# State products in 64x64 tiles from lasting token-major K buffers, with a new order of work

## The chip, the cores and the metric

One core of a Trainium2 chip runs the program. The metric is the device time of one execution in microseconds. Times are medians of repeated runs; the profile is one further execution.

## The reference

A complex gated recurrence over 768 tokens, for 4 batches and 8 heads of 48 features, feeds a gated feed-forward block that mixes tokens with a 768x768 matrix:

```python
def _attn_ref(q, k, v, a_re, a_im):            # each (4, 8, 768, 48)
    B, H, S, D = q.shape
    mag = np.sqrt(a_re * a_re + a_im * a_im)
    scale = np.minimum(mag, 0.999) / (mag + 1e-06)
    a_re_n, a_im_n = (a_re * scale, a_im * scale)
    for t in range(S):                         # S_re, S_im: (B, H, D, D), start at zero
        ar, ai = (a_re_n[:, :, t, :, None], a_im_n[:, :, t, :, None])
        new_re = ar * S_re - ai * S_im
        new_im = ar * S_im + ai * S_re
        kv = np.einsum('bhd,bhe->bhde', k[:, :, t], v[:, :, t])
        S_re, S_im = (new_re + kv, new_im)
        y[:, :, t] = np.einsum('bhd,bhde->bhe', q[:, :, t], S_re)
    return y

def _moe_ref(x, w_in, g_ln, w_sg, b_sg, w_out):   # x (4, 768, 384)
    h = gelu_tanh(x @ w_in)                       # w_in (384, 1024)
    u, v = (h[..., :512], h[..., 512:])
    v_n = (v - mean(v)) / np.sqrt(var(v) + 1e-06) * g_ln
    v_s = np.einsum('ts,bsd->btd', w_sg, v_n) + b_sg[None, :, None]   # w_sg (768, 768)
    return x + (u * v_s) @ w_out                  # w_out (512, 384)
```

## The kernel before

**The recurrence in chunks.** Each batch is cut into six chunks of 128 tokens, counted g = 0 to 23 over the four batches. The gates become logarithms and angles that are summed over time; then k and q are scaled and rotated with the sums, so that within a chunk the recurrence is a masked product of k and q, and across chunks a state of 96x48 numbers for each head (cosine and sine half of 48 features). Chunks are prepared in units of one or two: units 0 to 3 are batch 0, units 4 to 12 are the three units of each of the batches 1 to 3.

**The chains.** Each piece of work is a Python generator that issues one step of instructions at every `yield`. Of a unit n: `l`, `m` (loads of the gates; of k and q), `g` (`logs`), `e` (`scale`), `t` (`arctan`), `p` (`turns`), `s` (`sincos`). Of a chunk g: `v` (load of V into `vbuf[g % 2]`), `r` (`rotate`, line 557), `z` (`heads`, line 582), `c` (`tokens`, line 608), `d` (`states`, line 623), `a` (`attend`, line 653). Of the feed-forward block, for a batch b and a group of token chunks from c0: `nb_c0` (`normal`: x times the second half of `w_in` into `pv`, gelu, normalization), `xb_c0` (`expand`: the first half into `pu`, gelu), `yb_c0` (`spatial`: `w_sg` into `pvs`, gating, `w_out` into `po`, output). `w` prepares weights, `h` and `k` read gates and weights once more for a range check, `f` issues warming products into a tile that nobody reads (line 225), `o0`, `o1` and `ok` are constants, vectors and the end of the check.

**The order.** `ORDER` (line 32) is a table of tokens. `g2:3` calls the chain g2 three times; an apostrophe or two behind a token sets `alt`, which chooses the engine where a step has a choice: an elementwise step runs on GpSimd with one apostrophe and else on VectorE (`ew`, line 203); a copy out of PSUM on ScalarE without, on VectorE with one or two (`evac`, line 207); a rounding on ScalarE, GpSimd or VectorE (`high`, line 213); warming products are 0, 1 or 3. Every engine executes its instructions in the order of this table, and SyncE issues the DMAs in that order, each when what it needs is there. Nearly all DMAs are on SyncE's queue.

**From rotation to state, batches 1 to 3.** Data are feature-major. `rotate` makes two products for k and two for q (cosine and sine, lines 573 to 580) and writes each to DRAM (`rk`, `rq`). `heads` reads them back head by head into tiles `K` and `Q` of 96 rows, in four DMAs for a unit: K and Q of heads 0 to 3, K and Q of heads 4 to 7. `tokens` transposes K to token-major, four heads at a time into the PSUM tile `pk` (line 618), and copies it into a pool tile `kt` (line 620), of which there are two. In batch 0 data are token-major from the start: `rotate` writes `k0` into the same pool, and `heads` transposes.

**`states`** multiplies, for each head and each half of 64 tokens, K (64x96, stationary) by V (64x48) into `ps`; the two halves go to two PSUM tiles, and the last chunk of a batch needs the first half only (line 630). VectorE adds the older state (`Sm`, `S`), and `ew` scales the result (line 649). **`attend`** makes K times Q in tiles of 96x64 into `pa` (line 665), masks it to `am`, multiplies V by it in 64x64 tiles into two tiles `py` (line 680; row half, then column half, in turn), adds the states' part (line 689), copies `py` to `yp` (line 692) and writes it to DRAM. PSUM tiles `ps`, `pk`, `pa` and `py` share one pool of four banks (`pst`); the feed-forward block has three banks (`psm`).

Products of fp32 data show as two records on TensorE, those of rounded fp32 (fp32r) data as one; a transpose shows as one.

Of the kernel before, what the change touches and what calls it, by code (L numbers as in the profile page):

```python
# [37 lines left out]
w4 l4 g3 r2' g3:2 w5 a1:2 a0 r2'' w5:2 a1' a1 r3' m3 a1'' w12 w4 e3 g4 w4' w5 m3 w12 e3:2 e3' e3 z3 z3' z2 g4 z3 z2 z3
e3'' e3 z2:2 l6 a1 w12 p3 z2:4 v3 g4' p3' w12 g4 e3' e3 p3 d2:2 a2 d2 g4 a2 a2'' e3' t4 z3 z3'' z3 g4 p3:2 a2 p3:2
n0_0 v4 w12' a2 z3 l5 a3 n0_0' a3 a2 d2' p4:3 a2 d3 a2' a2 d3:2 n0_0' s3 a3' s3:2 w8 r5'' a3 r4 r4' a3 a3' a3 g4:2 g5  # L40
z5:2 z4 z4' z4 a3 z4:3 v5 r5' g4 d3' z4 z4'' e3 p4 z5:3 z5' p4 z5 a3 w3'' g5 o0 w11 e4 m4 z5' a5 a4' p4 l5 w8:2' a4 m4
n0_2 w12'' a4 d4' a5 d4 e4'' e4 a4 w3' s4:3 r6 e3 g5' g5 d4 n0_0 t5 e4' d4' w6 e4 r6 r6'' r6 a4 a4'' a4 d5 a4' a5''
# [20 lines left out]
d15 a15 d14' g11 v17 d15:2 g11:2 a15:4 z16:2 g11 z16:2 m10 g10 e10 y1_0 y1_3'' y1_3 c16 y1_3 c17 g11 c17' c17 c16''
c17' y1_3 a15 c16 c16' m10 x1_0 y1_3 e10'' y1_3 p10 y1_3 p10 y1_3 p10 y1_3 e10 y1_3 a16:3 d16 a16 d15 d16 n2_0 d16
s10:3 e9 a17 a16 a16' a17 e9'' a17'' a16 y1_0 d16' d17'' t11 d17'' r18'' a16 p11 a16 n2_0 r18 v18 a17:2 a17'' r18''
a17:3 h0 e10' p11 r18 n2_0' e10 r18'' r18 h0 r18' r18 p11 g11 y1_0 y1_0'' p11 y1_0' y1_0:2 g11 n2_3 h16 y1_0 z18 y1_0
# [968 lines left out]
```

## Time and profile before

| | us |
|---|---|
| runs of the kernel | 529.76, 521.91, 519.26; median 521.91 |
| profiled execution, its own time | 517.86 |
| its span, first to last instruction | 516.1 |
| TensorE busy | 459.8 |
| VectorE busy | 386.3 |
| ScalarE busy | 289.5 |
| GpSimd busy | 223.4 |

The span lies inside the execution's own time. Busy times are sums over the span, and a busy TensorE isn't TensorE at its peak, since its products are pipelined. In the rows, PE is TensorE, DVE VectorE, ACT ScalarE, POOL GpSimd and SP SyncE; L635 is line 635 of the kernel; `a<-b,c` names what is written and read.

### The profile page before, as it was taken

How to read it: one execution, taken by the hardware profiler on the slowest of the kernel's cores; microseconds unless marked ns; L12 is line 12 of the kernel's file. 1: busy time of each engine (PE TensorE's matmuls, PEld its weight loads, DVE VectorE, ACT ScalarE, POOL GpSimd, SP SyncE). 2: the span in 40 equal slices, each digit the busy share in tenths (PEclk: the TensorE clock that was granted, in tenths of full speed). 3: DMA queues.
4: the chain of work that ended last, by engine and by line, in shares of the span. 5: the costliest groups of instructions: out<-in, count | busy, mean ns of one | idle time of the engine just before them, and what ended most of it. 6: DMA issues, size and time to landing. Idle time of an engine off the chain costs nothing. (4 is left out here: it accounts for less than half of the span.)

```text
span 516.1 us, 11823 instructions
## 1 busy us (share of the span) xinstructions
PE 459.8 (89%) x4824; PEld 410.2 (79%) x4824; DVE 386.3 (75%) x607; ACT 289.5 (56%) x388; POOL 223.4 (43%) x250
## 2 busy tenths in 40 slices
PE   7799789879796989979898989999999969999995
PEld 4456677669695978868788989788999959889995
DVE  4999999996992966848878958889786823656644
ACT  7897779576975764395467463567755310253000
POOL 6447697667526025545616004547441312332102
PEclk9999789879896995989879999997999976999999
DMA  6885546891275784581671875977745793554232
GB/s 192 236 254 141 161 126 185 242 261 64 77 228 141 232 209 157 167 265 53 210 215 43 256 220 142 296 224 234 225 154 158 232 227 105 155 185 151 70 103 80
DMA packets 64148, 91.30 MB, mean 177 GB/s; under 512 B 9940, under 2 KB 49110, under 8 KB 64088
## 3 DMA queue, kind: packets, MB, share of 16 engines
q1 hardware_dynamic: 63944, 90.29, 59.2%
q8 instruction: 39, 0.64, 0.5%
q14 instruction: 21, 0.17, 0.1%
q10 hardware_dynamic: 144, 0.20, 0.1%
HBM read 66.87 MB, written 23.60 MB: 175 GB/s over the span
## 5 line engine op out<-in xcount | busy, mean ns | idle before, releaser
L197 ACT ACT_TABLE_LOAD x65 | 83.4, 1283 | 2.0 <-PEq L1020 0.9
L234 PE MATMUL pvs<-wsgh,vh 128*128 128x384 f32 x192 | 67.6, 352 | 2.8 <-DVE vh L220 2.8
L234 PE MATMUL pvs<-wsgh,vl 128*128 128x384 f32 x192 | 66.5, 346 | 0.2
L234 PE MATMUL pvs<-wsgl,vh 128*128 128x384 f32 x192 | 66.3, 345 | 0.0
L234 PEld LDWEIGHTS pvs<-wsgh,vh 128*128 128x128 f32 x192 | 37.4, 195 | 3.5 <-DVE vh L220 3.0
L618 PE MATMUL pk<-ident,K 96*128 96x96 f32 x144 | 20.0, 284 | 22.3 <-DMA K<-rk 22.3
L665 PE MATMUL pa<-Q,K 96*64 96x64 f32 x768 | 34.5, 251 | 5.4 <-DMA Q<-rq 4.7
L665 PEld LDWEIGHTS pa<-Q,K 96*64 96x64 f32 x768 | 30.4, 163 | 10.2 <-issue 4.2
L234 PEld LDWEIGHTS pvs<-wsgh,vl 128*128 128x128 f32 x192 | 37.4, 195 | 0.9 <-DVE vl L223 0.8
L234 PEld LDWEIGHTS pvs<-wsgl,vh 128*128 128x128 f32 x192 | 37.4, 195 | 0.0
L618 PEld LDWEIGHTS pk<-ident,K 96*128 96x128 f32 x144 | 16.2, 163 | 26.1 <-issue 15.1
L635 PE MATMUL ps<-vbuf,kt 64*96 64x48 f32 x528 | 34.3, 274 | 1.8 <-DVE kt L209 1.6
L635 PEld LDWEIGHTS ps<-vbuf,kt 64*96 64x96 f32 x528 | 31.9, 189 | 4.4 <-DVE kt L209 2.2
L234 PE MATMUL pu<-xh,winh 128*128 128x384 f32 x96 | 34.0, 354 | 0.6 <-DVE tg L818 0.6
L234 PE MATMUL pv<-winh,xh 128*128 128x512 f32 x72 | 31.9, 442 | 2.4 <-DVE tg L818 1.3
L805 PE MATMUL po<-gh,wouth 128*128 128x384 f32 x96 | 33.8, 352 | 0.0
L805 PE MATMUL po<-gl,wouth 128*128 128x384 f32 x96 | 33.2, 345 | 0.0
L805 PE MATMUL po<-gh,woutl 128*128 128x384 f32 x96 | 33.1, 345 | 0.0
L234 PE MATMUL pu<-xl,winh 128*128 128x384 f32 x96 | 33.1, 345 | 0.0
L234 PE MATMUL pu<-xh,winl 128*128 128x384 f32 x96 | 33.1, 345 | 0.0
L198 ACT ACTIVATE vr<-pv 128x512 f32<-128x512 f32 x24 | 14.4, 599 | 32.3 <-PE pv L234 25.8
L218 POOL TENSOR_SCALAR gh<-tg 128x384 fp32r<-128x384 f32 x14 | 8.2, 584 | 52.6 <-DVE tg L821 47.6
(290 smaller groups left out, 1262.0 us busy)
## 6 DMA issues: line engine op xcount, KB each, us to landing
K<-rk SPq DMA_DIRECT2D x18, 384.0 KB, 6.3
Q<-rq SPq DMA_DIRECT2D x18, 384.0 KB, 7.5
x<-xd SPq DMA_DIRECT2D x9, 576.0 KB, 5.6
vbuf<-in_v_dram SPq DMA_DIRECT2D x24, 192.0 KB, 2.6
xd<-yp SPq DMA_DIRECT2D x48, 96.0 KB, 2.6
gr<-in_f_re_dram SPq DMA_DIRECT2D x12, 384.0 KB, 3.3
gr<-in_f_im_dram SPq DMA_DIRECT2D x12, 384.0 KB, 4.7
out_dram<-x SPq DMA_DIRECT2D x23, 192.0 KB, 2.6
```

Of the source, the lines that this page charges most:

```text
L197: nc.scalar.preload_act_table_set(SETS[t])
L198: nc.scalar.activation(out, in_, func, scale=scale, **kw)
L218: nc.gpsimd.tensor_scalar(out=h, in0=src, scalar1=1.0, scalar2=1.0, op0=ALU.mult, op1=ALU.mult)
L234: nc.tensor.matmul(o, w(i), x(i), start=(i == 0 and j == 0), stop=(i == n - 1 and j == 2))
L618: nc.tensor.transpose(pk[:, hh, :], U[n]["K", i, g2][:, hh, :], ident[0:2 * D, 0:2 * D])
L635: nc.tensor.matmul(ps[:, h, :], kh(h)[r], V[r, h * D:(h + 1) * D], start=True, stop=True)
L665: nc.tensor.matmul(pa[r, h, :], K(h)[:, r], Q(h)[:, r], start=True, stop=True)
L805: nc.tensor.matmul(po[d], w[:, f, ds], g[:, f, :], start=f == 0 and j == 0, stop=f == NF - 1 and j == 2)
```

## The change

Token-major K gets two lasting buffers `kbuf`, 800 columns wide: 8 heads of 96 columns and 32 columns of zeros, filled once on GpSimd. `rotate` (batch 0) and `tokens` (other batches) write K of chunk g into `kbuf[g % 2]`. In `states` each product becomes two: the stationary operand is 64 tokens by 64 columns, first columns 0 to 63 of the head, then columns 64 to 127, of which the last 32 belong to the next head (or are the zeros). They go to rows 0 to 63 and 64 to 127 of `ps`, which has 128 rows; the adds read the first 96. `ORDER` is a new table over the same chains, with other apostrophes. Of the table, the diff shows the first lines and those around the unit 12 (chunks 22 and 23).

```diff
--- before.py
+++ after.py
@@ -30,57 +30,56 @@
 ORDER = """
-l0 g0 l0 g0 g0'' f'' w13 o0:2 g0 w0 g0 g0' t0 p0 g0:2 l2 w0:2 w13 w0 p0' p0 w13 s0 w13 e0 p0 l1 g1 l1 g1 g1'' w2:2
...
-a20 s12 a21 y2_3:7 d21 a21:2 d21 a21:3 y2_0 k3 y2_3:2 r22'' r22 a21 e12:2 x2_0 d21 r22:2 r22' r22 y2_0 r22' x2_0 r22
-v23 y2_0'' y2_0 y2_0'' n3_0 y2_0:2 d21 y2_0'' y2_0:2 z22 h22 f h14 f:5 h14 f y2_0:2 y2_0:2' y2_0:2 z22:2 h23:2 c22:2
-x2_0 z22 c22:2 c23 h21 c23'' c23:2 a22:3 d22 d23' d22:2 e12 h21 a22 k5 h11 h4 k5 e12' a23 x2_0 a23 a22 n3_0 a23 a22:4
...
+l0 g0 l0 w13 f' g0 g0'' g0:2 t0 o0:2 w13:2 f' w13 f g0' f'' w13'' f w0:4 w0:2'' g0:2 f' l1:2 p0:2 e0 w13'' p0:2 g1:2
...
+y2_3 v23 y2_3:7 r22' y2_3 e12' x2_0:6 e12 h21 y2_0 n3_0 h21 r22 r22'' r22 r22'' r22 r22'' r22 z22:4 y2_0 y2_0' y2_0''
+y2_0' y2_0 x2_0 h6 y2_0 y2_0'' y2_0 y2_0'' y2_0:2 h5 y2_0:2 y2_0'' x2_0 y2_0:2 a21:2 c22 c22'' c23 c22 c22'' c23:3 h5
+a22:2 e12 d22 a22'' a22:2 e12' y2_0 d22 a23 n3_0' d22 n3_0' a22' a23 a22 d22 d23' h13 a23'' a23:2 a22:2 h15 y2_0 d23'
...
 """

@@ -171,6 +170,11 @@
     for i in range(2):
         vbuf.append(cst([P, DM + 64 - D], F32, f"vbuf{i}"))
         nc.gpsimd.memset(vbuf[i][:, DM:], 0.0)
+    kbuf = []
+    for i in range(2):
+        kbuf.append(cst([P, 2 * DM + P - 2 * D], F32, f"kbuf{i}"))
+        nc.gpsimd.memset(kbuf[i][:, 2 * DM:], 0.0)
+    by_token = lambda g: kbuf[g % 2][:, 0:2 * DM].rearrange("p (h d) -> p h d", d=2 * D)
 
     cuts = SIZES0 + [[UC] * NU] * (B - 1)
     units = [(b, sum(z[:i]), z[i]) for b, z in enumerate(cuts) for i in range(len(z))]
@@ -561,9 +565,9 @@
         if not fea(n):
             by_heads = lambda t: t[:, i].rearrange("p (h d) -> p h d", d=D)
             for nm in "kq":
-                X = (ap_ if nm == "k" else mp).tile([P, H, 2, D], F32, tag={"k": "kt", "q": "x"}[nm], name=nm + "0", bufs=2)
+                X = by_token(g) if nm == "k" else mp.tile([P, H, 2 * D], F32, tag="x", name="q0", bufs=2)
                 u[nm + "0", i] = X
-                ew().tensor_mul(X, by_heads(u[nm]).unsqueeze(2).broadcast_to([P, H, 2, D]),
+                ew().tensor_mul(X.rearrange("p h (a d) -> p h a d", d=D), by_heads(u[nm]).unsqueeze(2).broadcast_to([P, H, 2, D]),
                                 u["csn"][:, :, i].rearrange("p a (h d) -> p h a d", d=D))
                 yield
             return
@@ -589,7 +593,7 @@
                     pk = pst.tile([2 * D, 4, P], F32, tag="t", name="pk")
                     stoke(pk[:, 0:2].rearrange("p a b -> p (a b)"))
                     for hh in range(4):
-                        nc.tensor.transpose(pk[:, hh, :], U[n][nm + "0", i][:, 4 * g2 + hh].rearrange("p a d -> p (a d)"), ident)
+                        nc.tensor.transpose(pk[:, hh, :], U[n][nm + "0", i][:, 4 * g2 + hh], ident)
                     yield
                     evac(X[:, 4 * g2:4 * g2 + 4, :], pk)
                     U[n][nm.upper(), i, g2] = X[:, 4 * g2:4 * g2 + 4, :]
@@ -610,8 +614,7 @@
         n, i = at_chunk[g]
         if not fea(n):
             return
-        kt_ = ap_.tile([P, H, 2 * D], F32, tag="kt", name="kt", bufs=2)
-        run["kt", g] = lambda h: kt_[:, h]
+        kt_ = by_token(g)
         for g2 in range(2):
             pk = pst.tile([P, 4, 2 * D], F32, tag="t", name="pk")
             for hh in range(4):
@@ -626,14 +629,17 @@
         c = g % NCH
         last = c == NCH - 1
         V = vbuf[g % 2]
-        kh = run["kt", g] if fea(n) else lambda h: U[n]["k0", i][:, h].rearrange("p a d -> p (a d)")
-        pss = [pst.tile([2 * D, H, D], F32, tag="t", name="ps") for _ in HALVES[:1 if last else 2]]
+        kb = kbuf[g % 2]
+        pss = [pst.tile([P, H, D], F32, tag="t", name="ps") for _ in HALVES[:1 if last else 2]]
         if g < EARLY:
             stoke(pss[0][:, 0:5].rearrange("p a b -> p (a b)"))
         for h in range(H):
             for ps, r in zip(pss, HALVES):
-                nc.tensor.matmul(ps[:, h, :], kh(h)[r], V[r, h * D:(h + 1) * D], start=True, stop=True)
-        yield
+                for w in HALVES:
+                    nc.tensor.matmul(ps[w, h, :], kb[r, h * 2 * D + w.start:h * 2 * D + w.stop], V[r, h * D:(h + 1) * D],
+                                     start=True, stop=True)
+        yield
+        pss = [ps[0:2 * D] for ps in pss]
         Sm = run["Sm", g] = ap_.tile([2 * D, H, D], F32, tag="Sm", name="Sm", bufs=1)
         if c == 0:
             evac(Sm, pss[0])
```

## Rows read from the trace of the kernel before

**Rows 1.** The page: busy time of each engine (us, share of the span, instructions), and the granted TensorE clock in 40 equal slices, in tenths; then span and mean granted clock of the core.

```profile
PE 459.8 (89%) x4824; PEld 410.2 (79%) x4824; DVE 386.3 (75%) x607; ACT 289.5 (56%) x388; POOL 223.4 (43%) x250
PEclk9999789879896995989879999997999976999999
core 0: 516.1 us, clock 0.912
```

**Rows 2.** A stretch of 40 us: its length, busy time (and instructions) of each engine, the granted clock, the DMA share and GB/s.

```profile
40.00:80.00 40.00, 33.42 (x458) 26.20 (x458) 37.61 (x46) 29.75 (x46) 31.12 (x27) 0.87 0.53 152
```

**Rows 3.** Waits, longest first in total: engine and line, what it waited for, us in total, times, longest; and the chain of work that ended last, by line, as shares of the span.

```profile
PE pk L618 <- DMA K<-rk: 22.3, 10, 3.8
PE pk L592 <- DVE yp L209: 4.2, 1, 4.2
by line: PE pvs L234 4.9%; DMA gr<-in_f_re_dram 3.6%; DMA K<-rk 3.2%; PE pu L234 3.2%; PE po L805 3.1%; PE pv L234 2.8%; PE ps L635 1.9%; issue 1.8%; DMA rq<-q 1.7%; PE pa L665 1.5%; DMA x<-xd 1.0%; POOL q L577 0.8%; PE py L689 0.8%; PE pk 
```

**Rows 4.** TensorE's timeline in one attention stage at full clock: start us, us, engine, line, operation, out<-in, shape, number of records.

```profile
308.27 1.15 PE L665 MATMUL pa<-Q,K 96*64 96x64 f32 x32
309.35 1.56 PE L635 MATMUL ps<-vbuf,kt 64*96 64x48 f32 x32
310.84 0.69 PE L680 MATMUL py<-am,vbuf 64*64 64x64 f32 x32
311.47 0.38 PE L493 MATMUL pd<-cols__3420,of_place 128*32 128x16 f32 x18
311.77 0.69 PE L665 MATMUL pa<-Q,K 96*64 96x64 f32 x16
313.75 1.55 PE L635 MATMUL ps<-vbuf,kt 64*96 64x48 f32 x16
315.23 0.69 PE L680 MATMUL py<-am,vbuf 64*64 64x64 f32 x32
```

**Rows 5.** Groups of instructions of TensorE by line and form: the products of `states` of batches 1 to 3 and of batch 0 (number of records | busy us, mean ns | idle before).

```profile
L635 PE MATMUL ps<-vbuf,kt 64*96 64x48 f32 x528 | 34.3, 274 | 1.8 <-DVE kt L209 1.6
L635 PE MATMUL ps<-vbuf,k 64*96 64x48 f32 x176 | 10.4, 253 | 0.9 <-DVE S L646 0.4 <-DVE k L566 0.3
```

**Rows 6.** TensorE's timeline: seven of the ten token transposes that waited for K, with the idle time before them in brackets (units 5, 5, 6, 7, 8, 12, 12).

```profile
157.30 0.55 PE L618 MATMUL pk<-ident,K 96*128 96x96 f32 x4 [1.75 <-DMA K<-rk]
160.79 0.90 PE L618 MATMUL pk<-ident,K 96*128 96x96 f32 x4 [2.95 <-DMA K<-rk]
194.81 1.51 PE L618 MATMUL pk<-ident,K 96*128 96x96 f32 x8 [3.79 <-DMA K<-rk]
228.67 0.90 PE L618 MATMUL pk<-ident,K 96*128 96x96 f32 x4 [3.72 <-DMA K<-rk]
259.08 0.88 PE L618 MATMUL pk<-ident,K 96*128 96x96 f32 x4 [1.70 <-DMA K<-rk]
417.23 0.52 PE L618 MATMUL pk<-ident,K 96*128 96x96 f32 x4 [2.13 <-DMA K<-rk]
422.21 2.15 PE L618 MATMUL pk<-ident,K 96*128 96x96 f32 x12 [2.49 <-DMA K<-rk]
```

**Rows 7.** The chain of work that ended last, in order of time (start us, us, what): four runs of dense products, with their number.

```profile
452.18 6.53 PE pv L234 x27
458.71 6.34 PE pu L234 x36
465.05 3.24 PE pvs L234 x18
486.54 6.33 PE po L805 x36
```

**Rows 8.** Four stretches after waits for K (columns as in rows 2).

```profile
160.00:170.00 10.00, 9.21 (x156) 8.66 (x158) 2.79 (x5) 6.68 (x8) 2.79 (x2) 0.52 0.35 103
194.00:208.00 14.00, 13.19 (x121) 12.75 (x122) 8.92 (x10) 6.45 (x8) 8.30 (x4) 0.53 0.50 167
228.00:235.00 7.00, 6.33 (x50) 5.82 (x50) 2.05 (x3) 4.12 (x6) 2.49 (x7) 0.54 0.69 229
256.00:265.00 9.00, 7.04 (x39) 6.83 (x38) 6.36 (x11) 3.26 (x6) 3.83 (x9) 0.50 0.72 224
```

**Rows 9.** Operations that the change moves or adds to: the copies of `yp` on VectorE and ScalarE and the fills of `vbuf` (ns min/median/max), the scaling of S on GpSimd (busy us, mean ns), and the first warming products (six records, three products).

```profile
L209 DVE COPY yp<-py x30: 392/412/429, 39.9 to 440.3; 128x256 f32<-128x256 f32 x30
L211 ACT COPY yp<-py x18: 351/372/377, 41.6 to 440.3; 128x256 f32<-128x256 f32 x18
L649 POOL TENSOR_TENSOR S<-S,dec 96x384 f32<-96x384 f32 x12 | 12.6, 1047 | 31.9 <-DVE dec L209 28.5 <-DVE S L646 1.9 <-PE pu L234 1.4
L173 POOL MEMSET vbuf<- x2: 114/114/114, 3.3 to 3.3; 128x16 f32 x2
2.82 2.93 PE L229 MATMUL warm<-u_turn,mask 128*128 128x256 f32 x6 [0.25 <-DVE cols L169]
```

**Rows 10.** DMA issues by line: KB each, median us to landing; the read back of K and the write of its second half.

```profile
K<-rk SPq DMA_DIRECT2D x18, 384.0 KB, 6.3
rk<-k SPq DMA_DIRECT2D x9, 384.0 KB, 2.8
```

More of the change, by code (lines that the diff above doesn't have):

```diff
@@ L38 @@
[L38 to L42, printed above, removed]
@@ L63 @@
[L63 to L66, printed above, removed]
-y1_0' y1_0:2 y1_0'' y1_0:2' y1_0:2 y1_0'' z18 p11 n2_0 y1_0'' m11:2 y1_0'' n2_0:6 z18 h9 z18 g11 n2_0 h16 n2_0 e11 h7
@@ new lines @@
+z4 a5 d3' z4 d4 a4:2 p4:2 a5 g5'' a4'' d4:2 e4'' e4 s4:2 a4 s4 m4 a5'' r6 a4:4 l6 o1 g5 t5 e4' g5 a5 a4 e4 r6 r6'' r6
+r6'' r6 d5' d4 a5:2 w15 d5'' n0_0 p5:3 n0_0'' a5:2 g6 g5 r6'' w15 n0_0 n0_0'' w15 n0_0' w8 e4 e4'' w8 a5 n0_3 g5 z6 g5
+n0_2'' w15' c6 w15' n0_2:3 n0_3:2 g5 g6 r6 w14 m5 z6:2 n0_0'' c6 w14 p5 e5 w14:2 n0_0'' e5' c7:2 e5 p5 w14:2 p5 n0_3'
+n0_3:2 z6 n0_3:3 n0_2' n0_3 c7 c6 n0_2 n0_2'' c6 a6:2 m5 v6 x0_3 e5' a6:2 c7' s5 g6' n0_3 s5 a6 d6 s5 n0_3:2 d6' w11
+l8 g6 t6 x0_3 d6 v7 w10 d6'' r8'' x0_3 w11 x0_3 a7:2 x0_0 r8 a7 a6 w10 a6 e5 r8:2 a6 r8'' r8 r8'' d7 n0_3'' n0_3
@@ new lines @@
+x0_3:2 d7 x0_3 w11 p6:2 n0_3:2'' n0_3 e5 r8 w10'' a7 e5 a7 n0_3'' a7' a7 n0_3'' n0_3:2 g6 p6:2 y0_3:2 g8 y0_3 g6:2
+y0_3' z8 m6 d7 z8:2 p6 y0_3' y0_3:2 x0_3 x0_0 g6 y0_3 l7 d7'' z8 v8 y0_3 l7 y0_3:3 m6 a7 c9 y0_3 c9 y0_3:2' g6 c9 c9'
+s6 y0_3 e6 f:3 v9 y0_3 c8:3 e6'' c8 a8:2 d8 e6 a8 d8 a7 a8:2 e6:2 y0_3' s6:2 a9:2 v10 l8 a8:4 a9 y0_3' r10'' r10 r10''
+r10:3 r10'' r10 y0_3' y0_3:7 d9 d8 d8'' a9 e6 y0_3 a9 g7:2 g7' d9:2 d9'' a9' g7:2 t7 g7 p7:2 e6 y0_3 p7 v11 g7 x0_0'
+a9 x0_0:5 p7 x0_0 z10:4 g7 a9 g7 a9 m7:2 p7:2 e7 y0_0 s7 y0_0:2 y0_0' c10 c10' c10:2 y0_0 x0_0 g8:2 a10:2 a11 d10 s7
@@ new lines @@
+g8 a10'' e7' l9 s7 d10 y0_0 l9 r12'' n1_0 a10 a11 d10 t8 v12 g8:2 r12 a10 a10'' a10 r12' e7 r12 e7' n1_0 y0_0:2 c11
+a10:2 a11 n1_0'' e7 r12 y0_0 d10' r12 r12' y0_0 r12 g8 y0_0:2 c11:3 n1_0 d11' a11 n1_0 a11 z12 d11' a11 g8 a11 z12:3
+g8 n1_0 p8:2 g9 e8 y0_0:2' x0_0 a11' a11 y0_0' y0_0:2 y0_0'' n1_0 l10 n1_3 n1_0 p8:2 c12 c12' c13 n1_0 y0_0:2' n1_0 p8
+n1_0 c12 c12' l10 n1_0:2 a12:2 m8 y0_0 f e8' a12'' c13'' c13 c13' g9 p8 g9'' n1_3'' n1_0 n1_0'' d12 e8 n1_3'' a12 g9
+y0_0:5 a12'' n1_0 y0_0 n1_0' n1_0 n1_0:2' n1_0 n1_0' y0_0 d12' n1_3 m8 e7 g9 v14 y0_0 e7' a13 f a13 s8:2 a12 d12 s8
@@ new lines @@
+p11 n2_0 p11 s11 c18 c18'' k8 s11 l12 e11'' c18 c18' m11 y1_0 g12' c19' c19 c19'' k8 y1_0 v19 s11 y1_0:5 n2_3 n2_0'
+y1_0:2 e11 n2_3'' n2_0'' n2_0' d18 n2_0'' n2_0 h14 d18' e10 a19:2 n2_0 a18:2 a18'' d18 n2_3:3 g12 h14 n2_3 n2_0''
+n2_0:2 n2_3:4 g12 r20' r20 r20'' x2_0 e11'' n2_3 a18 a18'' e10' a18 n2_3 x2_3 a18'' d18'' x2_3:5 r20 z20 a18 e11 r20''
+r20 a19 d19 a19 r20 d19 n2_3 a19 g12 a19' n2_3:2'' a19 n2_3' a19' n2_3 n2_3'' n2_3:2' n2_3'' h22 h11 t12 p12 g12 p12
+x2_3 c21 g12 x2_3 g12 e12 r20 y2_3 c21'' y2_3 y2_3'' y2_3:3 v20 c20 y2_3:2 y2_3'' h11' z20 y2_3' z20 y2_3:2 z20
@@ new lines @@
+a23 h13 a23 a23'' y2_0 n3_0 a23 h15 n3_3 n3_0:4 h22 k7 h18 n3_0:2 n3_3' n3_0 y2_0 n3_0:2 n3_0'' k7 n3_3 y2_0:8 h18
+n3_3 n3_0'' n3_0' n3_0:2'' n3_0:2' n3_3:2 k3 n3_0 k3 n3_0 k1 n3_3:4 k1 n3_3:4 x3_0 x3_3 k6:2 n3_3'' x3_3:6 n3_3:2''
+n3_3:2 n3_3:3'' y3_3 k9:2 y3_3 h20 y3_3 y3_3'' h6' y3_3' y3_3 x3_0'' h20 x3_3 x3_0'' h1 y3_3 h9 h1'' y3_3'' h17 f
+y3_3'' f y3_3'' y3_3:2 y3_3'' y3_3:2' y3_3:2 h4 y3_3:2 y3_3' x3_0:2 h17 h9 x3_0:2 h8 x3_0 h4'' h23 x3_0 y3_3:2 k12
+y3_3 h8 y3_3 k12 y3_3 k11 k0 k11 y3_3:2 y3_0 k0 y3_0 y3_0' y3_0'' y3_0' x3_0:2 k2:2 k10 y3_3:2 y3_0:9 y3_0'' y3_0 k5:2
@@ L84 @@
+y3_0 h23 h2 k10 y3_0:3 y3_0'' y3_0' y3_0:2 h2 h0 h19 y3_0:4 h0 y3_0:4 h19 ok:2
 """
```

57 lines of the change are left out of this document (20 added, 37 removed).

## The prediction

> **What bounds the kernel now.** I read the page's busy shares first, then the stretches of 40 us, the waits and the chain that ended last, and then TensorE's timeline in one attention stage. The reader is to see that TensorE is busy for 459.8 of 516.1 us and VectorE for 386.3, and that no other engine comes near them [rows 1]. Two losses lie on TensorE. It stands idle for 56 us; the largest wait with one cause is that of the token transposes for the K tiles that come back from DRAM, 22.3 us in ten waits [rows 3]. And the granted clock falls in places to the lower of its two levels (1.2 instead of 2.4 GHz): 0.87 on average from 40 to 80 us [rows 2], and single slices of the page stand at 5 or 6 tenths [rows 1]. The same DMA of K stands in the chain with 3.2% of the span, beside the dense products [rows 3]. From about 40 to 120 us VectorE is the second bound: 37.6 of 40 us busy in the first half of that [rows 2].
>
> **The products of `states`.** Now a chunk that isn't a batch's last has 16 products, shown as 32 records, and they take 309.35 to 310.84, 1.49 us [rows 4]. A last chunk uses only one row half: 8 products, 16 records, 313.75 to 315.23, 1.48 us [rows 4]. So two row halves cost what one does: they run beside each other. After the change each product becomes two of 64 columns, with four tiles of 64x64 in turn. The trace has this form already, in `attend`'s products with V: same tiles, same turn of the four tiles, weights of the same width, 64 columns streamed instead of 48. Those take 310.84 to 311.47, 0.63 us for 32 records, 19.7 ns each [rows 4]. With 64 records that gives 1.26 us, 0.23 less than now. A last chunk has 32 records in two column tiles, like the product of K and Q: 32 records from 308.27 to 309.35, 1.08 us [rows 4], 0.40 less. Twenty chunks at 0.23 and four at 0.40 are 6.2 us; the 704 records of today (528 and 176) become 1408 [rows 5]. TensorE is busy for 89% of the span [rows 1], so I count 5.5 us. The bounds: if column halves didn't overlap at all, a chunk would double, +1.48 for all 24 or a loss of 36 us; if the records came as fast as those of the small products into `pd` (18 records from 311.47 to 311.77 [rows 4], some 17 ns), a chunk would be 0.42 better and the sum a gain of 10. I take the middle because the form is the same.
>
> The Trainium skill speaks against this step: its page "TensorE: Matmul & The Clock Gate", section "Wait — 56ns, not 53.3ns?", says that starts of matmuls never come closer than about 25 ns however few columns they stream. By that, 64 records need 1.6 us, the chunks would lose 0.1 each, and the total would come out near 515. The trace disagrees: 19.7 ns in the 64x64 form [rows 4].
>
> **The lasting K buffers.** They replace a pool of two, chunk by chunk, so the depth of two stays. Two fills of 32 columns on GpSimd are new; the like of them for V took 0.114 us each [rows 9], at the start, where GpSimd is ahead. I cost them at nothing; without cover, 0.2 us. The second product of head 3 now reads 32 columns of head 4, which waits for the second copy out of PSUM somewhat earlier: between nothing and one copy, and nothing by the stream that follows.
>
> **The new order.** I walked both order tables step by step and gave each TensorE step its time: 6.53 us for 27 products into `pv`, 6.34 for 36 into `pu`, 3.24 for 18 into `pvs`, 6.33 for 36 into `po` [rows 7], and the small forms as above. Both orders run the stages in the same sequence; total TensorE work differs only by the products of `states` and by warming products (25 instead of 18; three in a row took 2.93 us at the lower clock [rows 9], so seven are 3 to 7 us, mostly where TensorE waits anyway: I charge 1).
>
> What differs is the lead of the token transposes. The write of K to DRAM takes 2.8 us and the read back 6.3 [rows 10]. Between a unit's last rotation of K and its first transposes there are now, in units 4 to 12, 6.4, 13.0, 13.0, 11.1, 15.3, 9.9, 16.3, 8.2 and 9.5 us of TensorE work; in the new order 6.6, 16.0, 17.6, 14.4, 18.1, 20.4, 16.2, 10.5 and 11.1: 103 becomes 131. Between the step that issues the second of the two reads of K and the transposes that need it there are now 6.1, 5.2, 0.0, 6.8, 4.7, 6.1, 7.2, 7.2 and 2.0 us, then 7.2, 6.8, 3.6, 8.2, 8.1, 7.2, 5.1, 3.2 and 11.9: 45 becomes 61. Unit 12 shows how: three groups of 18 into `pvs`, 3 x 3.2 us, become these and one group of 9 into `pu`, 1.6 more; and both reads, which stood among and behind them, move ahead of all of it. The waits today are 4.7 in unit 5 (1.75 and 2.95), 3.8 in 6, 3.7 in 7, 1.7 in 8 and 4.6 in 12 [rows 6]. By the growth of the leads 3.0, 3.6, 1.4, 1.7 and 3.0 of these can go, together 12.7. The work put ahead can itself be late, so I take half, 6 us. Bounds: a gain of 18.5 (the seven waits shown, all gone) and, since the second read of unit 11 gets 4.0 us less lead and Q in units 8 and 11 some 5 and 6 less, a loss of 5.
>
> **The clock.** Behind four of these waits (units 5 to 8) lie 40 us with a granted clock of 0.50 to 0.54 in which TensorE is busy for 35.8 [rows 8]; half of that, 18 us, is what the lower level costs there. I take a quarter, 4 us; bounds 0 and 18. What is late next is VectorE, which then sets when the rotations come.
>
> **Work that changes engine.** Of the counted moves the large ones are: 8 of 12 scalings of S go from GpSimd to VectorE (1.05 us each on GpSimd [rows 9]), 11 of 30 copies of `yp` go from VectorE to ScalarE (412 and 369 ns [rows 9]), and 9 of 18 rotations leave GpSimd. Over all moved steps, each at the mean of its group, VectorE ends with some 4 us more, ScalarE with some 15 more on its 289 [rows 1], GpSimd with some 40 less. `yp` copies free PSUM banks; on ScalarE they queue behind activations and table loads, and TensorE's next product into that pool waits. I charge 1.5, between a gain of 6 (VectorE less slowed beside GpSimd) and the loss of the second rival below.
>
> **Sum**, against the profiled execution's 517.86 us (span 516.1 and 1.8 around it): 5.5 + 6 + 4 - 1 - 1.5 = 13, which gives 504.9. The median of the runs, 521.91, is 0.8% above that execution, so the forecast is 509 us.
>
> **Rivals.**
> (a) The order brings nothing: what K waits for less, Q waits for more, and only the 5.5 stays: 512.4, scaled 516. For it: those shorter leads in units 8 and 11. Against: over the nine units the lead of Q, counted from its last rotation, rises from 142 to 160.
> (b) Slower: late copies on ScalarE. Each late `yp` holds a bank; the price is seen once now, 4.2 us of TensorE behind one such copy [rows 3], in a stretch whose clock is 0.87 [rows 2]; with the clock some 7 each. Two of the eleven moved copies eat the gain; four make it 533 on the profile, scaled 537. For it: ScalarE is 56% busy, in bursts. Against: the one case of today was a copy on VectorE, behind other work.
> (c) The 64x64 tiles overlap no better than pairs, at the 33.8 ns per record of K and Q [rows 4]: 64 records are 2.16 us, 0.67 more in twenty chunks and 0.40 less in four, a loss of 12 in place of the gain of 6, and the sum is 525. Against it: the 19.7 ns. The rule of the Trainium skill ("TensorE: Matmul & The Clock Gate", the section above) belongs here as its milder form, with 515.
> (d) More than forecast: VectorE, less disturbed beside a GpSimd with some 40 us less work, gains 6 in the first 120 us: 499, scaled 503, or 497 with more of the clock.
>
> **How the numbers follow.** Forecast 0.55 with its own range 500 to 517; (a) 0.20, (b) 0.12, (c) 0.04, (d) 0.07, and 0.02 for the kernel left as it is. Two per cent (10.4 us, about what a measurement of this kernel tells from no change) lies at 511.5. Of the forecast's 0.55, 0.43 is below it; with (d) faster has 0.50. The other 0.12, (a), (c) and the rest give 0.38, (b) 0.12. The range 495 to 526 leaves out (b) and the end of (d).
>
> **What would show it.** Right: 1408 records of 64x64 into `ps`, a chunk near 1.26 us at full clock; the waits of token transposes for K near 14 us in place of 22.3; fewer stretches at the lower clock, mean above 0.912 [rows 1]; GpSimd near 180 us. Wrong: a chunk of `states` at 1.5 us or more; TensorE waiting for `yp` or Q by 4 us several times; the waits for K unchanged. The forecast is wrong as a whole if the chunks are faster and the span isn't.

## The result, and the profile after

| | before | after |
|---|---|---|
| median of four runs (range), us | 523.67 (519.26 to 529.76) | 449.61 (447.83 to 451.73) |
| ratio, 95% interval | | 0.8612 (0.8532 to 0.8691) |
| profiled execution's own time, us | 517.86 | 447.83 |

Ratios, here and below, leave out disturbed runs, which the medians hold, so the two can differ by up to 1%. The change saves 74 us, 14%. 509 was forecast, 495 to 526 as the range: the sign was right, and the gain is more than five times the 13 us forecast. The page of the kernel after, and its core, against [rows 1]:

```profile
PE 414.9 (93%) x5542; PEld 372.7 (84%) x5542; DVE 352.2 (79%) x597; ACT 300.8 (67%) x418; POOL 195.6 (44%) x230
...
PEclk9999999969999999999999999999999999999998
core 0: 446.1 us, clock 0.986
```

Read it as a sum. TensorE's idle time, span less busy, was 516.1 - 459.8 = 56.3 us and is 31.2: 25 less. Its busy time falls by 45. The clock has two levels, 1.2 and 2.4 GHz, so a mean of 0.912 means that 2 x 0.088 x 516.1 = 91 us passed at the lower one, and 0.986 means 12. Half of what TensorE worked at the lower level is work that this level stretched. Before, at its mean busy share, that is an estimate of 40 us. After, it is about 2: most of the 12 us lie in a wait (91.86 to 102.10 us, below, with TensorE busy for 3.63). That is 38 of the 45. The other 7 fit the shorter products of `states` (12.4 us, below) less some 5 us more of warming products. VectorE is busy for 34 us less too, though it was given more to do: each instruction taken at the shortest time of its operation and shape, its work adds up to 344 us before and 350 after; as they ran, the same instructions took 418 and 382 (they overlap a little, so this is more than the busy time).

The windows, against [rows 2] (length, busy time and instructions of PE, PEld, DVE, ACT, POOL, granted clock, DMA share, GB/s):

```profile
40.00:80.00 40.00, 38.60 (x690) 30.25 (x686) 38.13 (x59) 37.96 (x56) 19.93 (x22) 1.00 0.70 198
...
91.86:102.10 10.24, 3.63 (x14) 3.19 (x15) 9.43 (x13) 9.92 (x13) 6.54 (x10) 0.50 0.88 266
```

From 40 to 80 us TensorE is busy for 5 us more than before and the clock stays up; GpSimd does 19.9 us of work where it did 31.1. The second line is the one place, but for the last 3 us of the span, where the clock still falls: it falls during the longest wait that is left, which ends at 98.47, and is back after 3.6 us of work. The waits, and TensorE's timeline at that place, at one chunk of `states`, at the last chunk of batch 3 and at unit 12 (against [rows 3, 4, 6]):

```profile
PE pk L621 <- DMA K<-rk: 10.2, 3, 8.6
```

```profile
98.47 1.51 PE L621 MATMUL pk<-ident,K 96*128 96x96 f32 x8 [8.61 <-DMA K<-rk]
...
304.32 1.15 PE L639 MATMUL ps<-vbuf,kbuf 64*64 64x48 f32 x64
305.29 0.66 PE L686 MATMUL py<-am,vbuf 64*64 64x64 f32 x32
...
358.44 0.74 PE L621 MATMUL pk<-ident,K 96*128 96x96 f32 x7
...
365.70 1.08 PE L639 MATMUL ps<-vbuf,kbuf 64*64 64x48 f32 x30
366.56 0.27 PE L686 MATMUL py<-am,vbuf 64*64 64x64 f32 x2
366.61 0.23 PE L639 MATMUL ps<-vbuf,kbuf 64*64 64x48 f32 x2
366.67 0.65 PE L686 MATMUL py<-am,vbuf 64*64 64x64 f32 x30
```

A chunk's 64 records take 304.32 to 305.29, 0.97 us where it was 1.49 [rows 4]; a last chunk's 32 take 365.70 to 366.67, 0.97 us as well, where it was 1.48. And the same event stands at different times: unit 12's first transposes start at 358.4 instead of 417.2 [rows 6], 59 us earlier and behind the same amount of products into `pvs` and `po`, but unit 4's, here at 98.47, stood in the kernel before at

```profile
97.30 0.55 PE L618 MATMUL pk<-ident,K 96*128 96x96 f32 x4 [0.66 <-DMA K<-rk]
```

So unit 4's transposes come no earlier, and the time is gained behind them. The other engines are ahead by then all the same. The windows up to 98.4 us, before and then after:

```profile
0.00:98.40 98.40, 82.86 (x972) 60.54 (x973) 85.43 (x118) 77.07 (x110) 66.26 (x93) 0.93 0.65 191
...
0.00:98.40 98.40, 80.14 (x1173) 59.10 (x1173) 85.51 (x134) 87.71 (x128) 58.08 (x90) 0.97 0.69 202
```

VectorE and ScalarE have run 262 instructions where it was 228. How much of the later gain rests on this lead, no run shows.

Three groups, against [rows 5, 9] (busy us, mean ns, idle before): the products of `states` in their new form, and the scalings of S, of which four are left on GpSimd.

```profile
L639 PE MATMUL ps<-vbuf,kbuf 64*64 64x48 f32 x1408 | 27.5, 220 | 0.0
...
L655 DVE TENSOR_TENSOR S<-S,dec 96x384 f32<-96x384 f32 x16 | 11.7, 731 | 0.2
...
L655 POOL TENSOR_TENSOR S<-S,dec 96x384 f32<-96x384 f32 x4 | 3.3, 826 | 8.0 <-ACT dec L215 7.6 <-DVE S L652 0.4
```

### The profile page after: what moved, and what is told of

It reads as the page before. It is cut to its first block, busy times and chain, and to the rows that moved or that the text cites. A ratio compares the mean times of both kernels' runs of the same rounds, so it can differ in the third digit from the quotient of the medians.

```text
span 446.1 us, 13263 instructions
## 1 busy us (share of the span) xinstructions
PE 414.9 (93%) x5542; PEld 372.7 (84%) x5542; DVE 352.2 (79%) x597; ACT 300.8 (67%) x418; POOL 195.6 (44%) x230
## 4 chain that ended last, share of the span: by engine, by line
PE 67%; DMA 12%; DVE 8%; POOL 5%; ACT 4%; issue 3%; SPq 1%; DVEq 0%; POOLq 0%
PE pvs L238 18%; PE po L811 10%; PE pu L238 10%; PE pv L238 7%; PE pa L671 5%; PE ps L639 4%; DMA K<-rk 4%; PE py L695 4%; PE pk L621 3%; DMA rq<-q 2%; PE py L686 2%; DMA xd<-yp 2%; DMA Q<-rq 2%; DMA raw<-in_moe_w_out_dram 1%; POOL nt L719 1%
## 5 line engine op out<-in xcount | busy, mean ns | idle before, releaser
L238 PE MATMUL pvs<-wsgl,vh 128*128 128x384 f32 x192 | 64.6, 336 | 0.0
L222 POOL TENSOR_SCALAR gh<-tg 128x384 fp32r<-128x384 f32 x14 | 14.2, 1011 | 51.2 <-DVE tg L827 39.7
L227 POOL TENSOR_TENSOR gl<-tg,gh 128x384 fp32r<-128x384 f32 x18 | 21.8, 1211 | 28.6 <-DVE gh L224 22.5
L238 PE MATMUL pv<-winh,xh 128*128 128x512 f32 x72 | 30.2, 420 | 0.1
L671 PE MATMUL pa<-Q,K 96*64 96x64 f32 x768 | 28.3, 225 | 2.0 <-DMA Q<-rq 1.2
L824 DVE SCALAR_TENSOR_TENSOR tg<-pvs,gcol,bsg 128x384 f32<-128x384 f32 x32 | 19.6, 612 | 13.2 <-PE pvs L238 13.0
L671 PEld LDWEIGHTS pa<-Q,K 96*64 96x64 f32 x768 | 24.7, 138 | 4.9 <-issue 1.5
L238 PE MATMUL pv<-winh,xl 128*128 128x512 f32 x72 | 28.7, 398 | 0.0
L238 PE MATMUL pv<-winl,xh 128*128 128x512 f32 x72 | 28.6, 397 | 0.0
L202 ACT ACTIVATE gh<-tg 128x384 fp32r<-128x384 f32 x12 | 6.2, 521 | 33.0 <-DVE tg L827 33.0
```

The source lines that it names most:

```text
L202: nc.scalar.activation(out, in_, func, scale=scale, **kw)
L222: nc.gpsimd.tensor_scalar(out=h, in0=src, scalar1=1.0, scalar2=1.0, op0=ALU.mult, op1=ALU.mult)
L227: ew().tensor_tensor(out=l, in0=src, in1=h.bitcast(F32), op=ALU.subtract)
L238: nc.tensor.matmul(o, w(i), x(i), start=(i == 0 and j == 0), stop=(i == n - 1 and j == 2))
L671: nc.tensor.matmul(pa[r, h, :], K(h)[:, r], Q(h)[:, r], start=True, stop=True)
L824: nc.vector.scalar_tensor_tensor(out=tg, in0=pv, scalar=gcol[:, f:f + 1], in1=bsg[:, tsl], op0=ALU.mult, op1=ALU.add)
```

## The experiments

Ratios are to the kernel before, run on the same chip. Costs below are differences of medians where no other is named: of variants of the kernel before to that kernel on the same chip (521.9 to 525.7), of variants of the kernel after to its 449.61. "Idle" is span less TensorE's busy time and "lower" is 2 x (1 - mean clock) x span, both from the profiled execution, us.

| run | median | ratio (95% interval) | idle | lower | VectorE busy | GpSimd busy |
|---|---|---|---|---|---|---|
| before | 523.67 | 1 | 56.3 | 91 | 386.3 | 223.4 |
| after | 449.61 | 0.8612 (0.8532 to 0.8691) | 31.2 | 12 | 352.2 | 195.6 |
| e1, new tiles, old order | 512.44 | 0.9862 (0.9747 to 0.9977) | 66.1 | 70 | 384.1 | 225.2 |
| e2, old tiles, new order | 450.89 | 0.8635 (0.8497 to 0.8772) | 17.7 | 20 | 353.0 | 186.4 |
| e3, after, old engines | 521.87 | 1.0038 (0.9989 to 1.0087) | 73.0 | 61 | 378.2 | 228.8 |
| e4, after, old sequence | 539.33 | 1.0342 (1.0240 to 1.0443) | 86.9 | 95 | 365.2 | 184.6 |
| e5, after, unit 4's K earlier | 448.38 | 0.8614 (0.8533 to 0.8695) | 26.5 | 19 | 350.6 | 198.5 |
| e6, before, TensorE kept at work | 512.21 | 0.9887 (0.9761 to 1.0013) | 41.1 | 59 | 380.6 | 222.8 |
| e7, after, old copies | 466.09 | 0.8966 (0.8855 to 0.9077) | 34.8 | 35 | 354.7 | 188.0 |
| e8, after, old leads | 488.83 | 0.9411 (0.9327 to 0.9495) | 52.5 | 54 | 357.2 | 195.4 |
| e9, after, old elementwise engines | 516.61 | 0.9877 (0.9815 to 0.9940) | 66.5 | 74 | 381.0 | 229.1 |
| e10, before, reads ahead | 549.30 | 1.0511 (1.0432 to 1.0591) | 78.9 | 116 | 380.8 | 220.7 |
| e11, before, K not waited for | 514.08 | 0.9835 (0.9776 to 0.9894) | 53.0 | 73 | 385.6 | 223.1 |
| e12, after, K not waited for | 450.72 | 0.8591 (0.8528 to 0.8655) | 29.5 | 21 | 350.6 | 190.5 |
| e13, before, K and Q not waited for | 505.25 | 0.9663 (0.9563 to 0.9762) | 48.6 | 74 | 384.7 | 224.5 |
| e14, after, K and Q not waited for | 447.69 | 0.8538 (0.8464 to 0.8612) | 27.8 | 16 | 355.3 | 200.2 |
| e15, after, old choice in feed-forward | 487.60 | 0.9304 (0.9221 to 0.9387) | 50.7 | 41 | 370.9 | 201.1 |
| e16, after, old choice in the recurrence | 485.08 | 0.9274 (0.9179 to 0.9368) | 50.1 | 45 | 360.4 | 219.5 |
| e17, before, short GpSimd products | 505.43 | none | 49.9 | 80 | 358.1 | 157.0 |
| e18, after, short GpSimd products | 442.15 | 0.8461 (0.8370 to 0.8553) | 20.9 | 14 | 341.4 | 131.8 |

Not all came out as expected. e3, e4, e9 and e10 were slower than every range that was expected of them, e12 by 0.7 us; e2 was faster; e7, e16 and e18 lay between two.

### Which part: tiles or order

**e1.** The kernel after with the table of the kernel before.

```diff
 ORDER = """
-l0 g0 l0 w13 f' g0 g0'' g0:2 t0 o0:2 w13:2 f' w13 f g0' f'' w13'' f w0:4 ...
+l0 g0 l0 g0 g0'' f'' w13 o0:2 g0 w0 g0 g0' t0 p0 g0:2 l2 w0:2 ...
```

> The new tiles and buffers under the old order table. Theory 'order' (the new order keeps TensorE fed, and the granted clock then stays at its upper level): only the shorter products show, 24 chunks at some 0.5 us, about 12 us off 523.7, so 508 to 516, with the stretches at the lower clock (92 us in all before) still over 70 us. Theory 'tiles' (the four small tiles are what keeps the clock up): below 470, clock above 0.97 under the old order too.

**e2.** The kernel before with the table of the kernel after (the same lines, exchanged).

> The new order table over the old products (64x96, pool of two). Theory 'order': 455 to 465 (449.6 plus 24 chunks at 0.5 us and little else), clock above 0.97. Theory 'tiles': 505 to 515, clock near 0.92.

Measured 512.4 and 450.9. The tiles alone are worth 7 us by the ratio and 11 by the medians, the order alone 71 and 73, which is all of it: e2 and the kernel after can't be told apart. The page of e2:

```profile
PE 430.1 (96%) x4838; PEld 387.4 (87%) x4838; DVE 353.0 (79%) x597; ACT 301.1 (67%) x418; POOL 186.4 (42%) x228
core 0: 447.8 us, clock 0.978
```

and its timeline at unit 4's first transposes:

```profile
97.95 1.51 PE L617 MATMUL pk<-ident,K 96*128 96x96 f32 x8 [3.15 <-DMA K<-rk]
```

Under the new order the shorter products turn into waiting: TensorE is busy for 15 us less with the tiles (414.9 for 430.1) and idle for 13.5 more. 5.5 of that is this one wait, 8.61 us with the tiles and 3.15 without, ending at 98.5 and 98.0 us.

### Sequence or engines

**e3.** The kernel after with its own sequence, but each step with the apostrophes that it has in the old table. They differ in 294 of 1628 calls, and in 205 of them the step runs on another engine; in the others the step has no choice, or both marks choose the same engine.

```diff
-... r0'' v0 g1:2 e0 e1 r0'' w7 p1'' w7' l2 ...
+... r0'' v0 g1:2 e0 e1 r0 w7 p1'' w7' l2 ...
```

> New tiles and the new sequence of steps, but each step with a choice of engine runs where the old table put it (warming products stay with the sequence). If the sequence carries the gain: 450 to 465. If it is the choice of engines (less on GpSimd, copies of yp on ScalarE): 490 to 515. A split in two halves would be near 480.

**e4.** The reverse: the kernel after with the old sequence and each step on its new engine (the same calls), here against the old table.

```diff
-... w13 w0 p0' p0 w13 s0 ...
+... w13 w0 p0:2 w13 s0 ...
```

> New tiles and the old sequence of steps, with the new table's choice of engine for each step. If the sequence carries the gain: 500 to 515, about as the tiles alone. If the choice of engines does: 450 to 470.

With e1 and the kernel after this is a square, all four with the new tiles: old sequence and old engines 512 (0.986), new engines alone 539 (1.034), new sequence alone 522 (1.004), both 450 (0.861). Neither half alone brings anything; the gain comes when both are there. The first waits of TensorE in e3, then in e4:

```profile
PE phi L535 <- ACT im L202: 5.7, 2, 3.5
PE py L695 <- DVE Sm L647: 5.7, 4, 2.6
PE pv L238 <- ACT vr L202: 4.4, 1, 4.4
```

```profile
PE pk L621 <- DMA K<-rk: 14.4, 9, 3.2
PE py L695 <- DVE Sm L647: 10.7, 4, 7.7
PE pu L238 <- ACT vr L202: 6.8, 2, 5.3
```

e3 has no wait for the K read back from DRAM among its first, and is as slow as the kernel before: waits spread over many producers, three of them shown, take the place of one large one.

### Parts of the order, undone one at a time

**e7.** 47 copies out of PSUM back on the engine of the old table.

```diff
-... a0:2 d0' p1 a0' a0 d0 ...
+... a0:2 d0 p1 a0' a0 d0 ...
```

> The changed kernel with the copies out of PSUM (K, kt, Sm, yp, dec: 47 of them change) back on the engine that the old table gave them; all else as in the changed kernel. If these copies carry the fit between sequence and engines: above 490 (with all choices old it was 521.9). If the elementwise and rounding steps do: below 465.

**e8.** Rotations and reads of K later, so that the leads of the transposes are those of the old order or less (95 us in sum; 103 before, 131 after).

```diff
-y0_3' z8 m6 d7 z8:2 p6 y0_3' y0_3:2 x0_3 x0_0 ...
+y0_3' m6 d7 p6 y0_3' y0_3 z8:3 y0_3 x0_3 x0_0 ...
```

> The changed kernel with the rotations of units 4 to 12, and the reads of K behind them, moved later in the table, so that the TensorE work between a unit's last rotation of K and its first transposes is 95 us in sum, as in the old order (103), in place of 131. Theory 'the lead of K is the gain': the waits for K come back (15 us or more), stretches at the lower clock with them, 480 or more. Rival 'the fit of the whole order': 452 to 465.

**e9.** 149 elementwise and rounding steps that had changed engine go back; the copies stay, and so do nine steps (six of the range check `h`, three of `turns`).

```diff
-... r0'' v0 g1:2 e0 e1 r0'' w7 ...
+... r0'' v0 g1:2 e0 e1 r0 w7 ...
```

> The changed kernel with all elementwise and rounding steps back on the engine that the old table gave them, and the copies out of PSUM as in the new one. With all choices old it was 521.9, with the copies alone old 466.1. If the costs add up, some 500 to 510; if the two choices only hurt together, below 475.

**e15, e16.** e9 in two: the 99 steps of weights and feed-forward (108 in the expectation, which counts the nine that stay), and the 50 of the recurrence (9 scalings of S and, in batches 1 to 3, 10 rotations back on GpSimd among them).

```diff
-... g0' f'' w13'' f w0:4 ...          (e15)
+... g0' f'' w13' f w0:4 ...
-... a5 g5'' a4'' d4:2 ...             (e16)
+... a5 g5' a4 d4:2 ...
```

> The changed kernel with the old choice of engine for the elementwise and rounding steps of the feed-forward block and the weights (108 steps change engine). If cost goes with the number of steps: 485 to 500 here, 465 to 475 in the next. If it hangs on the recurrence's steps, which feed K and Q: below 470 here.

> The changed kernel with the old choice of engine for the recurrence's elementwise steps (50 change, among them 9 scalings of S and 10 rotations that go back to GpSimd). By number of steps 465 to 475; if K and Q carry it, 490 or more, with waits for K, Q or S of 10 us and more.

Against the kernel after they cost 16 (e7), 39 (e8), 67 (e9), 38 (e15) and 35 (e16). The halves of e9 add up to somewhat more than e9, and the 50 steps of the recurrence cost as much as the 99 others. The parts together, 16 + 39 + 67, are more than the whole: their costs overlap. First waits of e8, and of e9:

```profile
PE pk L621 <- DMA K<-rk: 26.4, 9, 7.0
```

```profile
PE pk L621 <- DMA K<-rk: 9.7, 3, 8.4
PE pa L671 <- DVE Q L213: 5.1, 2, 4.9
PE pv L238 <- ACT vr L202: 3.7, 1, 3.7
```

In e8 the waits for K come back, and 16 us more of them cost 39, as the first theory had it. But the edit goes past the old order: walked in the prediction's way, the leads behind the second reads of K are estimated at some 29 us in sum, where the old order has 45 and the new one 61. So the 39 us may overstate what the new leads are worth. In e9 they are as short as in the kernel after (9.7 and 10.2), and 67 us are lost all the same: the leads of K matter, but don't explain the gain.

### One wait taken out

**e11, e13.** The kernel before with token transposes that read a constant, and with products of K and Q that do as well. **e12, e14.** The same in the kernel after.

```diff
-nc.tensor.transpose(pk[:, hh, :], U[n]["K", i, g2][:, hh, :], ident[0:2 * D, 0:2 * D])
+nc.tensor.transpose(pk[:, hh, :], mask[0:2 * D, :], ident[0:2 * D, 0:2 * D])
+        if fea(n):                                  # e13, e14 only, in attend
+            K = Q = lambda h: mask[0:2 * D, :]
```

> The kernel before, with the token transposes of batches 1 to 3 reading a constant tile instead of K (so the states' K is left out of the result); reads, copies and all else stay. Theory 'the waits for K carry half of the gain': 475 to 495, lower clock under 50 us. Rival 'other waits take their place in the old order': 508 to 520.

> The kernel before; in batches 1 to 3 the token transposes and the products of attend read a constant tile instead of K and Q (both left out of the result; reads, copies and all else stay). Theory 'late K and Q as a whole': 470 to 495. Rival 'the fit of all steps': 498 to 512, with other waits (kt, S, x, xh) in their place.

> The same on the changed kernel (the states' K is left out of the result). The new order has one wait for K left, 8.6 us in unit 4; as its removal by an earlier read brought nothing: 444 to 450 by both theories. Below 440 would say that the leads still bind.

> The same on the changed kernel (K and Q left out of the result): 443 to 451, since hardly any such wait is left there. The distance to e13 is what the new order is worth apart from the arrival of K and Q.

In the kernel before, K gives back 9 us and K with Q 18, of 74. With neither waited for in either kernel, they are still 58 us apart (505.25 and 447.69): by this measure some 16 of the 74 hang on when K and Q arrive. First waits of e11, of e13 and of e12:

```profile
PE pa L665 <- DMA Q<-rq: 19.2, 7, 4.6
```

```profile
PE ps L635 <- DVE kt L209: 9.8, 3, 6.7
PE pk L592 <- DVE yp L209: 4.3, 1, 4.3
PE pvs L234 <- DVE vl L223: 3.0, 3, 1.4
```

```profile
PE pv L238 <- ACT xh L202: 6.5, 1, 6.5
PE pa L671 <- DMA Q<-rq: 3.7, 3, 1.9
```

22.3 us of waiting for K [rows 3] become 19.2 for Q, and without Q the next is the copy `kt`. In the kernel after it is the same on a smaller scale: `xh` takes the place of K and nothing is gained.

**e10.** The kernel before with the reads of K and Q called right behind the rotations.

```diff
-... r6 r6'' r6 a4 a4'' a4 d5 ... a5:2 z6 a5'' a5 ...
+... r6 r6'' r6 z6 a4 a4'' a4 d5 ... a5:2 a5'' a5 ...
```

> The kernel before; the reads of K and Q of units 4 to 12 stand right behind the writes that they read, so that the TensorE work between the step that issues a read and the transposes is the whole lead from the rotation (6 to 23 us in place of 0 to 13). Theory 'reads stood too late in SyncE's queue': waits for K below 10 us, 490 to 505. Rival 'the rotation itself is late, or what is put behind the waiting reads is': 515 to 530.

**e5.** In the kernel after, unit 4's first read of K called ahead of a write of `yp` and a load of x that stand before it on SyncE's queue.

```diff
-r6'' r6 d5' d4 a5:2 ... g5 z6 g5
+r6'' r6 z6 d5' d4 a5:2 ... g5:2
```

> The changed kernel with one step moved: in unit 4 the first read of K stands ahead of the write of yp and of the load of x on SyncE's queue, not behind them (read now issued at 94.0 us, though K was written at 83.6). Theory 'queue': the read lands some 7 us earlier, the wait of 8.6 us and most of the 10 us at the lower clock behind it go, 449.6 becomes 437 to 444. Rival 'something else is late anyway': 448 to 451.

**e6.** The kernel before with 56 products, overwritten before anything reads them, in front of the eight groups of transposes that wait, so that TensorE isn't idle there.

```diff
+            for _ in range(FILL.get((g, g2), 0)):
+                nc.tensor.matmul(o, mask, u_turn[:, 0:4 * D], start=True, stop=True, skip_group_check=True)
```

> The kernel before with 56 products that nobody reads (each some 0.35 us at the upper clock) ahead of the eight groups of token transposes that waited longest for K, and nothing else. They only fill time in which TensorE waited. Theory 'the clock costs by itself': stretches at the lower clock fall from 92 us to under 50, and the time falls with it by 10 to 25 us, to 499 to 513. Theory 'the lower clock is a result of lateness elsewhere': the clock rises but TensorE then waits longer for the same reads, 518 to 528.

e10 is 27 us slower, with these first waits:

```profile
PE pk L618 <- DMA K<-rk: 14.4, 7, 4.4
PE pvs L234 <- DVE tg L818: 8.1, 2, 4.4
PE ps L635 <- DVE kt L209: 6.7, 2, 6.5
```

K waits less, and what shares the queue and the order with it more. e5 does what it should at its place, with the read issued at 87.1 instead of 94.0 us and K's waits at 0.5 us, and gains nothing:

```profile
PE pv L238 <- ACT xh L202: 4.6, 1, 4.6
```

e6 takes 32 us off the time at the lower clock and 15 off the idle time, and saves 6 us by the ratio, 10 by the medians, with an interval that just includes none. This decides less than was hoped: 512.2 lies within the first theory's range by 1 us, and the time at the lower level fell to 59 us, not under 50. At the busy share, 32 us are 14 us of stretched work, of which some 6 to 10 came back. In proportion the 79 us that the change takes away would be worth 15 to 25 of 74. That proportion holds is not shown, and the added products may themselves hold up the transposes behind them.

### Does GpSimd slow VectorE?

**e17, e18.** In the kernel before and after, six products that GpSimd may do (rotations, scalings of S and others) cover 8 columns of the last axis when they run on GpSimd, and are whole on VectorE.

```diff
+    def few(t):
+        if alt[0] != 1:
+            return t
+        return t[(slice(None),) * (len(t.shape) - 1) + (slice(0, 8),)]
-                ew().tensor_mul(t, x, by)
+                ew().tensor_mul(few(t), few(x), few(by))
```

> The kernel before; the in-place products on GpSimd (scalings of q, k and S, rotations, im, gating; 55 steps, some 88 us) work on 8 columns of the last axis only, so most of their result is left out. Theory 'GpSimd's long steps, and VectorE slowed beside them, are what the old order loses': VectorE busy below 365, 475 to 495. Rival 'order of dependences whatever the durations': VectorE falls too, but 505 to 515.

> The same in the changed kernel (most of the result of the same kinds of step on GpSimd is left out). If its order has already hidden GpSimd's steps: 443 to 450. Below 440 would say that they still cost time there.

e17's four runs are 494.4, 504.2, 506.7 and 508.9 beside 518.7 to 526.8 of the kernel before; they spread by 3%, so there is no interval. By the medians some 20 us are gained in the kernel before (10 to 32 by single runs) and 7 in the kernel after; 505 is where the rival's range begins. The page of e17 (its run of 506.7), and then two groups of VectorE's, a rotation's product `em` and the lower half `vl` of a rounded v, in the kernel before and in e17 (ns min/median/max, first and last start):

```profile
PE 455.1 (90%) x4824; PEld 409.6 (81%) x4824; DVE 358.1 (71%) x607; ACT 289.5 (57%) x388; POOL 157.0 (31%) x250
```

```profile
L577 DVE TENSOR_TENSOR em<-k,csn x5: 948/1165/3275, 86.3 to 401.4; 128x768 f32<-128x768 f32 x5
...
L223 DVE TENSOR_TENSOR vl<-vr,vh x15: 666/693/4898, 128.7 to 467.1; 128x512 fp32r<-128x512 f32 x15
```

```profile
L582 DVE TENSOR_TENSOR em<-k,csn x5: 946/955/3277, 84.3 to 392.3; 128x768 f32<-128x768 f32 x5
...
L228 DVE TENSOR_TENSOR vl<-vr,vh x15: 661/692/1087, 123.3 to 456.2; 128x512 fp32r<-128x512 f32 x15
```

VectorE executes the same 607 instructions in e17 as before, none of them changed, and is busy for 28 us less: in the kernel before the longest `vl` took 4.9 us, in e17 1.09, and the median `em` 1.17 and 0.96. Above the shortest time of each operation and shape, VectorE's instructions add up to 74 us in the kernel before, 44 in e17 and 33 in the kernel after. The timelines of GpSimd and of VectorE at two of the longest steps in the kernel before show how:

```profile
199.89 4.96 POOL L223 TENSOR_TENSOR xl<-x,xh 128x1152 fp32r<-128x1152 f32 x1
...
350.97 0.83 POOL L649 TENSOR_TENSOR S<-S,dec 96x384 f32<-96x384 f32 x1
351.75 1.83 POOL L470 TENSOR_TENSOR q<-q,ep 128x768 f32<-128x768 f32 x1
353.53 1.85 POOL L577 TENSOR_TENSOR em<-k,csn 128x768 f32<-128x768 f32 x1
```

```profile
201.41 0.95 DVE L465 TENSOR_TENSOR k<-k,em 128x768 f32<-128x768 f32 x1
202.40 3.27 DVE L577 TENSOR_TENSOR em<-k,csn 128x768 f32<-128x768 f32 x1
...
351.04 4.90 DVE L223 TENSOR_TENSOR vl<-vr,vh 128x512 fp32r<-128x512 f32 x1 [0.56 <-POOL vh L218]
```

`vl` begins behind the scaling of S, and ends half a microsecond after three GpSimd products in a row have ended (355.38): read so, it waits for all three and then does its work (0.67 where nothing delays it). `em` begins beside GpSimd's `xl` and ends 0.82 after it. The Trainium skill says this ("SBUF — State Buffer", section "SBUF: two separate sides"): a VectorE instruction with two inputs in SBUF and a GpSimd instruction that reads SBUF hold a port pair in turn, each for its whole length. The trace agrees. `xl` isn't among the shortened products, and the longest `em` stays at 3.3 us in e17.

The 20 us hold two things at once, VectorE's shorter steps and GpSimd's results that come sooner. And VectorE's busy time is now near that of the kernel after (358 and 352), but the old order is still 55 us slower than the new one with the same tiles (e2): this is a part of what the order avoids, not all.

## Why the prediction was wrong

**Products of `states`: the mechanism right, the size half.** 1408 records in the form foreseen, but 0.97 us a chunk instead of 1.26, 15 ns a record instead of the 19.7 taken from `attend` [rows 4]. A last chunk took 0.97 for 1.08. The sum is 24 chunks at 0.52 = 12.4 us instead of 6.2, a little past the upper bound of 10. (That bound took 0.42 for last chunks too; at its own rate they would save 0.95, and the sum would be 12.) Alone it shows (e1, 7 to 11 us); under the new order it can't be seen in the time. The Trainium skill ("TensorE: Matmul & The Clock Gate", section "Wait — 56ns, not 53.3ns?") has starts never closer than about 25 ns. The 15 ns contradict it for this form.

**The order: the step that failed.** It was priced as leads of one wait, the growth of 28 us between rotation and transposes, worth 6 with a bound of 18.5. As bookkeeping even the unhalved number was right: 12.7 was the working's sum, and the waits for K fell by 12.1 (22.3 to 10.2). That is partly luck, since 8.6 of the 10.2 left are a wait of unit 4 that the working didn't have. And they are not where most of the gain comes from: taken out altogether they return 9 us (e11), and with their leads kept 67 are lost (e9). What the runs showed in place of the 6 us is 73 for the order alone (e2), which neither its sequence (e3) nor its engine choices (e4) bring alone. I treated each wait as a sum to be removed. In these runs it is the place where the lateness of several producers is paid, and it is paid elsewhere if that place closes (Q in e11, `kt` in e13, `xh` in e12). So the upper bound was no bound: the seven waits shown and the 18 us of clock make 36, and the order brought 73.

**The clock: a quarter of four stretches.** 4 us were charged and 18 taken as the bound, from the stretches behind four waits [rows 8], about 40 us. The mean clock gave 91 us at the lower level all along [rows 1]; 79 of them are gone, worth some 38 of TensorE's busy time by the estimate above. In the table the time at the lower level goes with the idle time (20 and 17.7 us in e2, 95 and 86.9 in e4), so it couldn't be forecast apart from it. e6 speaks against the clock as the main cause: with 32 us less at the lower level, the time fell by 6 to 10.

**Engines: the sign for VectorE wrong.** "Some 4 us more" came out as 34 less, though the work itself grew by 6 at the shortest times (344 to 350). The means of the groups held steps that were waiting for GpSimd (e17), and in the kernel after more than half of the time above the shortest is gone (74 us to 33). GpSimd has 28 us less (40 said), ScalarE 11 more (15 said). The charge of 1.5 was no price at all: with the old sequence the new engines cost 27 us (e4 against e1), with the new sequence they save 72 (the kernel after against e3). Costing the moves by themselves had no chance of seeing this. The warming products took 5 us more of TensorE's time (16.4 for 11.3); what of it cost anything, against the charge of 1, can't be told apart.

**The rivals.** (a) fell: the order brought nearly everything. (b) fell: no wait for `yp` is among TensorE's first, and putting copies back costs 16 (e7). (c) fell with the 0.97 us; its loss of 12 gives a sum of 522, scaled 527, not 525. (d) named the right engine pair, and had 0.07, but it set the gain of 6 in the first 120 us: unit 4's transposes, at 98 us, come no earlier. Shortening GpSimd's products gave the kernel before some 20 us (e17).

**What stays open.** No single part explains the order. Which of its 205 changed engine choices and of its moved steps are needed was split only into copies, two halves and leads; their costs overlap (122 for 73). Whether a run of e17's kind with the lengthening fully gone would return more wasn't tried.
